# Decode-attention forward: the engines' order taken from the scheduler and written by hand, with three heads in flight

## Chip, cores, metric

One Trainium2 chip (trn2), one core. The metric is the device time of one launch in microseconds (us). An execution that is over 1.5% above the fastest of its kernel would be set aside as slow. The profile is one execution of the same program; its span is about 2 us shorter than the timed launch.

The engines are named as the profile names them: PE (matmul; PEld are its weight loads), DVE (vector), ACT (scalar), POOL, SP (it issues the loads). "DMA share" is the mean busy share of the core's 16 DMA engines.

## The reference, cut to what matters

A conditioned layer norm, one decode step of attention over a long cache, an MLP, and the gradients of all of it. Only the attention's forward is touched by the change: 32 heads, one query token, a cache of 8192 keys and values of 192 numbers per head, in bf16.

```python
q = (h @ wq) per head                            # 32 heads x 192
scores = einsum(q, k_cache) * 192 ** -0.5        # 8192 per head
p = softmax(scores)
o = einsum(p, v_cache)                           # 192 per head
x = x + ga * (o @ wo)
# then an MLP block, and vjp: gradients for k_cache, v_cache, wq, wo, w3, w4, ...
```

K and V are 201 MB together and are read once in the forward. The gradients of K and V are as large again; they are written by the backward, which reads V a second time.

## The kernel before

Per head, 8192 keys lie as 128 partitions x 64. The forward of a head has these steps; the line numbers are those that the profile shows.

```python
def dot_mul(src, vec, halve, psR):                         # half of a head's K
    prod = pp.tile(...)                                    # ONE buffer of 12 KB per partition
    V_.tensor_tensor(out=prod, in0=src, in1=vec, op=mult)              # L266, DVE 3.36 us
    V_.tensor_tensor(out=prod[lo], in0=prod[lo], in1=prod[hi], op=add) # L270, DVE 1.75 us
    ps = psR.tile(...)
    for k in range(0, w, TS):                              # "the tree": 6 matmuls, 1.4 us
        T_.matmul(ps, lhsT=ident_bf, rhs=prod[:, :, k:k+TS], ...)      # L273, PE
    return ps

def softmax(h, S_h):        # reduce_max m1 (DVE), max matmul mx (PE), negm (DVE),
    ...                     # E4 = exp(S_h + negm) and two copies (ACT, 1.0 us)

def scale_v(q, v, E4, Ef):  # vs = E * V for a quarter of the keys: 7 of 16 rows on ACT
    ...                     # (2.6 us with a small copy), 9 of 16 on DVE (1.05 us)

def m_quarter(q, kb, vs, mp, op):   # PE, 2.7 us: mp += K^T vs (L330, L334), op += 1^T vs (L338)

for i in range(HQ + 1):                          # program text, not yet the engines' order
    # ... loads of head i; mp, op for head i-1
    if new: d0 = dot_mul(kh[0], qh, True, psR)
    quarter(0)                                   # scale_v and m_quarter of head i-1
    if new: d1 = dot_mul(kh[1], qh, True, psR); dot_sum(d0, ...)
    quarter(1)
    if new: dot_sum(d1, ...); E4, Ef = softmax(i, S_h)
    quarter(2); quarter(3)
    # every 4th head: q_chunk (the next 4 heads' q) or mod_blocks; 10 such chunks in all
    if old: m_out(...)                           # copies of mp, op (ACT), one add (DVE)
            # every 2nd head: pair_out (10 small fp32 matmuls into po, reciprocal rz,
            # 15 matmuls ao_ps, copy AO on ACT) and e_rows (a transpose, a copy, a store)
```

A scheduling layer decides in which order these instructions stand on each engine. PE, DVE and ACT then take them in that order: the Trainium skill, "TensorE: Matmul & The Clock Gate", Part 1 ("Engine queue depths"), calls ACT's and DVE's queues strict FIFO and says that PE can pull weight loads ahead of matmuls.

Of the kernel before, what the change touches and what calls it, by code (L numbers as in the profile page):

```python
# [8 lines left out]
FP32 = mybir.dt.float32  # L9
BF16 = mybir.dt.bfloat16  # L10
ALU = mybir.AluOpType
# [9 lines left out]
def kernel(  # L21
# [26 lines left out]
    nc = tc.nc  # L48
# [62 lines left out]
    def tcol(n, name, dtype=FP32):  # L111
        return tmp.tile([P, n], dtype, name=name)
# [147 lines left out]
        nc.sync.dma_start(out=v, in_=V_hd[h][:, t * JH : (t + 1) * JH, :])  # L260
        return v

    def dot_mul(src, vec, halve, psR):

        prod = pp.tile([P, JH, DH], BF16, name="prod", tag="prod")
        V_.tensor_tensor(out=prod, in0=src, in1=vec[:, None, :].to_broadcast([P, JH, DH]), op=ALU.mult)  # L266
        w = DH
        if halve:
            w //= 2
            V_.tensor_tensor(out=prod[:, :, 0:w], in0=prod[:, :, 0:w], in1=prod[:, :, w : 2 * w], op=ALU.add)  # L270
        ps = psR.tile([P, JH, TS], FP32, name="dot_ps")
        for k in range(0, w, TS):
            T_.matmul(ps, lhsT=ident_bf, rhs=prod[:, :, k : k + TS], start=(k == 0), stop=(k == w - TS))  # L273
        return ps

    def dot_sum(ps, dst):
        V_.reduce_sum(out=dst, in_=ps, axis=AX.X)  # L277
# [5 lines left out]
    with tc.tile_pool(name="kp", bufs=1) as kp, tc.tile_pool(name="vs", bufs=3) as vsp, tc.tile_pool(name="ft", bufs=2) as ft, \  # L283
# [9 lines left out]
            nc.sync.dma_start(out=kb, in_=K_hd[h][:, t * JH : (t + 1) * JH, :])  # L293
            return kb

        def softmax(h, S_h):
            m1 = tcol(1, "m1")
            V_.reduce_max(out=m1, in_=S_h, axis=AX.X)
            mx = psB.tile([P, P], FP32, name="mx", tag="b")
            T_.matmul(mx, lhsT=m1[:, 0:1].to_broadcast([P, P]), rhs=ident_f, start=True, stop=True)  # L300
            negm = tcol(1, "negm")
            V_.reduce_max(out=negm, in_=mx, axis=AX.X, negate=True)
            E4 = ft.tile([P, J, 4], BF16, name="E4")
            A_.activation(out=E4, in_=S_h[:, :, None].to_broadcast([P, J, 4]), func=ACT.Exp, bias=negm[:, 0:1], scale=1.0)
            A_.copy(out=E_all[:, h, :], in_=E4[:, :, 0])
            Ef = ft.tile([P, J], FP32, name="Ef")
            A_.copy(out=Ef, in_=E4[:, :, 0])
            return E4, Ef
# [28 lines left out]
                p0 = 32 * (k % 4)  # L337
                T_.matmul(op[p0 : p0 + 32, 0:MW], lhsT=ones_bf, rhs=vs[:, k, 0:MW], start=(q == 0 and k < 4), stop=(z and k >= JQ - 4), skip_group_check=True)  # L338

        def m_out(h, mp, op):  # L340
            t, b = divmod(h, 2)
            A_.copy(out=M1[:, h, :], in_=mp[:, 0:MW])  # L342
            mt = ft.tile([P, MW], FP32, name="mt", bufs=1)
            A_.copy(out=mt[64:128, :], in_=mp[64:128, MO : MO + MW])
            V_.tensor_tensor(out=M2[64 * b : 64 * b + 64, t, :], in0=mp[0:64, MO : MO + MW], in1=mt[64:128, :], op=ALU.add)
            osb = ft.tile([P, MW], FP32, name="osb")
            A_.copy(out=osb, in_=op[:, 0:MW])
            return osb

        def e_rows(t):  # L350
            ps = psS.tile([P, P], BF16, name="er_ps", tag="s")
            T_.transpose(out=ps[0 : 2 * J, :], in_=E_all[:, 2 * t : 2 * t + 2, :].rearrange("p h j -> p (h j)"), identity=ident_bf)
            er = ft.tile([P, P], BF16, name="er", bufs=1)
            A_.copy(out=er[0 : 2 * J, :], in_=ps[0 : 2 * J, :])
            nc.scalar.dma_start(out=eT_d[2 * t * J : (2 * t + 2) * J, :], in_=er[0 : 2 * J, :])

        def pair_out(t, os2, wo_t):

            po = psS.tile([P, 8], FP32, name="po", tag="s")
            for b in range(2):  # L360
                rows = slice(64 * b, 64 * b + 64)
                for k in range(3):
                    T_.matmul(po[rows, k : k + 1], lhsT=os2[b][:, k:DH:3], rhs=c32[:, 0:1], start=True, stop=True)
                T_.matmul(po[rows, 3:4], lhsT=c32[:, 0:64], rhs=os2[b][:, DH:MW], start=True, stop=True)
                T_.matmul(po[:, 4 + b : 5 + b], lhsT=c32, rhs=os2[b][:, DH:MW], start=True, stop=True)
            rz = tcol(3, "rz")
            V_.reciprocal(out=rz, in_=po[:, 3:6])
            V_.tensor_scalar(out=o_col[:, 3 * t : 3 * t + 3], in0=po[:, 0:3], scalar1=rz[:, 0:1], scalar2=None, op0=ALU.mult)
            V_.tensor_copy(out=rinv[:, 2 * t : 2 * t + 2], in_=rz[:, 1:3])
            o2 = ft.tile([P, 3, 2], BF16, name="o2")  # L370
            V_.tensor_tensor(out=o2, in0=omask, in1=o_col[:, 3 * t : 3 * t + 3, None].to_broadcast([P, 3, 2]), op=ALU.mult)
            ps = psS.tile([P, ND, 2], FP32, name="ao_ps", tag="s")
            for i in range(ND):
                for k in range(3):
                    T_.matmul(ps[:, i, :], lhsT=wo_t[:, k, i * P : (i + 1) * P], rhs=o2[:, k, :], start=(k == 0), stop=(k == 2))
            A_.copy(out=AO[:, :, 2 * t : 2 * t + 2], in_=ps)

        st, os_, wo_l = {}, {}, {}
        q_chunk(0, load_w(wq_v, 0, CW))
        mb = MB0  # L380
        for i in range(HQ + 1):
            new, old = i < HQ, i > 0
            if new:
                kh = [load_k(i, 0), load_k(i, 1)]
                vh = [load_v(i, 0)]
                S_h = ft.tile([P, J], FP32, name="S_h")
                qh = qs_bc[:, i * DH : (i + 1) * DH]
                if i % 2 == 0:
                    wo_l[i // 2] = load_wo(i // 2)
            if old:  # L390
                pk, pv, pE4, pEf = st.pop(i - 1)
                mp = psM.tile([P, 512], FP32, name="mp")
                op = psO.tile([P, 256], FP32, name="op")

            def quarter(q):
                if old:
                    m_quarter(q, pk[q // 2], scale_v(q, pv[q // 2], pE4, pEf), mp, op)

            if new:
                d0 = dot_mul(kh[0], qh, True, psR)  # L400
            quarter(0)
            if new:
                d1 = dot_mul(kh[1], qh, True, psR)
                dot_sum(d0, S_h[:, 0:JH])
            quarter(1)
            if new:
                vh.append(load_v(i, 1))
                dot_sum(d1, S_h[:, JH:J])
                E4, Ef = softmax(i, S_h)
                st[i] = (kh, vh, E4, Ef)  # L410
            quarter(2)
            quarter(3)
            if i % 4 == 3 and i + 1 < HQ:
                q_chunk((i + 1) // 4, load_w(wq_v, ((i + 1) // 4) * CW, ((i + 1) // 4 + 1) * CW))
            if i % 4 == 1 and mb < NMB:
                nb = min(CW // P, NMB - mb)
                mod_blocks(mb, nb, load_w(wm_v, mb * P, (mb + nb) * P))
                mb += nb
            if old:
                os_[i - 1] = m_out(i - 1, mp, op)  # L420
                if i % 2 == 0:
                    t = (i - 2) // 2
                    pair_out(t, (os_.pop(i - 2), os_.pop(i - 1)), wo_l.pop(t))
                    e_rows(t)
        while mb < NMB:
            nb = min(CW // P, NMB - mb)
            mod_blocks(mb, nb, load_w(wm_v, mb * P, (mb + nb) * P))
            mb += nb
    V_.tensor_tensor(out=dbo, in0=dy_c, in1=gb, op=ALU.mult)


# [123 lines left out]
    with tc.tile_pool(name="bk1", bufs=1) as bk1, tc.tile_pool(name="ob", bufs=4) as ob, tc.tile_pool(name="bst", bufs=1) as bst:  # L555
# [166 lines left out]
        for h in range(HQ):  # L722
            doh = do_bc[:, h * DH : (h + 1) * DH]
            qh = qs_bc[:, h * DH : (h + 1) * DH]
            for t in range(2):
                js = slice(t * JH, (t + 1) * JH)
                v = load_v(h, t)
                dP = tcol(JH, "dP")
                dot_sum(dot_mul(v, doh, False, psR), dP)
                dS4 = bst.tile([P, JH, 4], BF16, name="dS4", bufs=2)  # L730
                V_.scalar_tensor_tensor(
                    out=dS4,
                    in0=dP[:, :, None].to_broadcast([P, JH, 4]),
                    scalar=cpr[:, h : h + 1],
                    in1=E_all[:, h, js, None].to_broadcast([P, JH, 4]),
                    op0=ALU.subtract,
                    op1=ALU.mult,
                )
                dV = ob.tile([P, JH, DH], BF16, name="dV", tag="o")
                outer_v(dV, load_er(h, t), doh)  # L740
                nc.gpsimd.dma_start(out=dV_hd[h][:, js, :], in_=dV)  # L741
                dK = ob.tile([P, JH, DH], BF16, name="dK", tag="o")
                times(dK, qh, dS4, 0, JH)
                nc.gpsimd.dma_start(out=dK_hd[h][:, js, :], in_=dK)
                for f in side.get(2 * h + t, ()):
                    f()
# [35 lines left out]
```

## Time and profile before

| | before |
|---|---|
| median, 4 runs | 1719.45 us (1716.70 to 1722.35) |
| forward: last copy of the last head ends | 780.2 us |
| mean time between two heads' negm | 23.5 us |
| backward: from its first multiply to the end | 873.4 us |

The windows view of the kernel before. The columns are the stretch, its length, the busy us of each engine with its number of instructions, the granted PE clock (1.00 is full), the DMA share and GB/s:

```profile
26.00:762.00 736.00, 603.10 (x7102) 409.15 (x7101) 512.96 (x468) 390.51 (x1225) 0.00 (x0) 0.86 0.74 295
839.40:1712.80 873.40, 657.67 (x4095) 228.18 (x4093) 559.41 (x665) 478.72 (x651) 91.32 (x158) 0.59 0.96 386
```

In the forward (first line) no engine is full: PE is busy 82%, DVE 70%, ACT 53%, and the loads have a share of 0.74. The backward (second line) is bound by its transfers at a share of 0.96. So the time that an order can win lies in the forward.

The waits view of the forward before, 30 to 762 us: who waited for whom, us in total, times, longest (S_h is the tile of the head's scores):

```profile
DVE prod L266 <- PE dot_ps L273: 121.9, 31, 5.3
DVE S_h L277 <- PE dot_ps L273: 46.9, 32, 2.8
DVE negm L302 <- PE mx L300: 21.4, 31, 1.0
...
ACT M_212 L342 <- PE mp L334: 148.2, 31, 6.5
ACT AO L376 <- PE ao_ps L375: 66.3, 15, 6.7
```

DVE waits 3.9 us a time for a tree before it may overwrite the one product buffer. The timeline of DVE shows why, for one head (start, length, then the wait in brackets):

```profile
302.64 0.29 DVE L302 TENSOR_REDUCE negm<-mx 128x1 f32<-128x128 f32 x1 [0.89 <-PE mx L300]
303.51 3.00 DVE L316 TENSOR_TENSOR vs<-v_sb,E_3592 128x1728 bf16<-128x1728 bf16 x3 [0.58 <-ACT E_3592 L304]
306.42 3.35 DVE L266 TENSOR_TENSOR prod<-KB_237,qs_bc 128x6144 bf16<-128x6144 bf16 x1
...
310.66 1.75 DVE L270 TENSOR_TENSOR prod<-prod 128x3072 bf16<-128x3072 bf16 x1
316.26 3.36 DVE L266 TENSOR_TENSOR prod<-KB_238,qs_bc 128x6144 bf16<-128x6144 bf16 x1 [3.85 <-PE dot_ps L273]
```

and on PE the tree that it waits for, which could have begun at 312.4:

```profile
304.71 1.77 PE L330 MATMUL mp<-vs,KB_240 128*128 128x193 bf16 x10
...
311.98 1.52 PE L330 MATMUL mp<-vs,KB_241 128*128 128x193 bf16 x16
...
314.76 1.46 PE L273 MATMUL dot_ps<-prod,ident_bf 128*128 128x512 bf16 x6
```

The tree stands behind M quarters of the head whose softmax has just ended. The first of them began at 304.71, a microsecond after the scaling of V did (303.51), and the scaling had waited for that softmax. One head's chain (softmax, scaling, M) and the next head's chain (multiply, fold, tree) are thus tied into one loop; DVE and PE cannot run ahead of each other.

### The profile page before, as it was taken

The numbers are of one execution on the slowest core, as the hardware profiler recorded it, in microseconds if no ns is written. First come the engines' busy times: TensorE is split into PE (matmuls) and PEld (weight loads), VectorE is DVE, ScalarE is ACT, GpSimd is POOL, SyncE is SP. The second block draws the span as 40 slices with busy tenths as digits, with TensorE's granted clock in tenths as the row PEclk, the third lists the DMA queues.
The fourth block names the chain that finished last, engine by engine and source line by source line (L and its number), as shares of the span: only waits on it lengthen the run. The fifth ranks groups of instructions, "written<-read, shape, count | busy, mean of one in ns | idle before, by whom it ended". The sixth has DMA issues, their size and how long they took to land.

```text
span 1712.8 us, 28289 instructions
## 1 busy us (share of the span) xinstructions
PE 1311.6 (77%) x11811; PEld 675.5 (39%) x11811; DVE 1114.0 (65%) x1273; ACT 900.0 (53%) x1948; POOL 99.9 (6%) x177
## 2 busy tenths in 40 slices
PE   4888778888888888786558587887678888878774
PEld 2555555555555655555223132232222222222211
DVE  5666666767767776764557566666756666666664
ACT  2455544555555555553456365555555555555554
POOL 0000000000000000000101010111010101010111
PEclk9888878888888888886667665556665555555555
DMA  8787577777787777765489999999999999999988
GB/s 347 321 324 309 226 315 279 295 280 295 283 324 307 292 286 286 288 235 201 178 353 414 379 382 409 396 400 424 424 377 402 392 405 369 373 397 396 409 342 336
DMA packets 78270, 576.00 MB, mean 336 GB/s; under 512 B 9374, under 2 KB 27118, under 8 KB 37182
## 3 DMA queue, kind: packets, MB, share of 16 engines
q1 hardware_dynamic: 51530, 347.23, 51.2%
q0 software_dynamic: 23776, 225.92, 32.2%
q8 instruction: 92, 1.51, 0.4%
q10 hardware_dynamic: 2836, 1.05, 0.2%
q14 instruction: 36, 0.29, 0.0%
HBM read 347.74 MB, written 226.43 MB: 335 GB/s over the span
## 4 chain that ended last, share of the span: by engine, by line
PE 40%; issue 23%; DVE 14%; DMA 12%; ACT 7%; POOL 2%; SPq 0%; POOLq 0%; ACTq 0%; DVEq 0%
PE dot_ps L273 14%; PE mp L330 10%; DVE prod L266 7%; DMA v_sb<-in_A_v_cache_dram 4%; PE mp L334 4%; PE op L338 3%; PE dv_ps L682 3%; ACT vs L323 3%; DVE prod L270 3%; DMA w_st<-in_A_wq_dram 2%; ACT dV L683 2%; PE wT_ps L573 2%; DMA wo_st<-in_A_wo_dram 2%; DMA w_st<-in_w_mod_dram 1%; DVE S_h L277 1%
## 5 line engine op out<-in xcount | busy, mean ns | idle before, releaser
L273 PE MATMUL dot_ps<-prod,ident_bf 128*128 128x512 bf16 x1152 | 475.0, 542 | 87.1 <-DVE prod L270 46.6
L683 ACT CAST dV<-dv_ps 128x768 bf16<-128x768 f32 x512 | 388.2, 811 | 205.7 <-PE dv_ps L682 186.6
L323 ACT ACTIVATE vs<-v_sb,Ef 128x192 bf16<-128x192 bf16 x896 | 325.8, 448 | 0.0
L682 PE MATMUL dv_ps<-do_bc,er_b 1*128 1x192 bf16 x2048 | 219.6, 324 | 64.8 <-ACT dV L683 64.0
L273 PEld LDWEIGHTS <-ident_bf 128*128 128x128 bf16 x1152 | 119.4, 117 | 264.7 <-issue 233.9
L266 DVE TENSOR_TENSOR prod<-v_sb,do_bc 128x6144 bf16<-128x6144 bf16 x64 | 214.3, 3349 | 3.5 <-ACT do_bc L624 3.5
L277 DVE TENSOR_REDUCE dP<-dot_ps 128x32 f32<-128x512 f32 x64 | 44.2, 691 | 235.5 <-PE dot_ps L273 235.5
L682 PEld LDWEIGHTS <-er_b 1*128 1x128 bf16 x2048 | 65.2, 102 | 300.5 <-issue 296.7
L270 DVE TENSOR_TENSOR prod<-prod 128x3072 bf16<-128x3072 bf16 x64 | 112.0, 1750 | 0.0
L338 PE MATMUL op<-vs,ones_bf 128*32 128x193 bf16 x2048 | 102.6, 264 | 0.0
L573 PE MATMUL wT_ps<-ident_bf,w_st 128*128 128x128 bf16 (+1 forms) x470 | 50.7, 285 | 66.4 <-ACT wqT L574 25.8
L342 ACT COPY M_212<-mp 128x193 f32<-128x193 f32 x32 | 10.3, 322 | 152.5 <-PE mp L334 152.5
L574 ACT COPY wqT<-wT_ps 128x1024 bf16<-128x1024 bf16 (+1 forms) x52 | 50.6, 973 | 49.2 <-PE wT_ps L573 35.1
L277 DVE TENSOR_REDUCE S_h<-dot_ps 128x32 f32<-128x512 f32 x64 | 44.0, 688 | 46.9 <-PE dot_ps L273 46.9
L741 POOL DMA_DIRECT2D out_dram<-dV x64 | 35.4, 553 | 658.2 <-ACT dV L683 635.1
L573 PEld LDWEIGHTS <-w_st 128*128 128x128 bf16 (+1 forms) x470 | 36.8, 130 | 86.5 <-issue 47.5
L266 DVE TENSOR_TENSOR prod<-KB_238,qs_bc 128x6144 bf16<-128x6144 bf16 x13 | 43.6, 3355 | 28.8 <-PE dot_ps L273 23.9
L338 PEld LDWEIGHTS <-ones_bf 128*32 128x32 bf16 x2048 | 43.4, 96 | 46.4 <-issue 29.0
L266 DVE TENSOR_TENSOR prod<-KB_241,qs_bc 128x6144 bf16<-128x6144 bf16 x13 | 43.6, 3356 | 27.4 <-PE dot_ps L273 27.4
L266 DVE TENSOR_TENSOR prod<-KB_239,qs_bc 128x6144 bf16<-128x6144 bf16 x13 | 43.6, 3356 | 27.3 <-PE dot_ps L273 27.3
L330 PE MATMUL mp<-vs,KB_238 128*128 128x193 bf16 x416 | 52.6, 275 | 10.6 <-DVE vs L316 6.3
L330 PE MATMUL mp<-vs,KB_240 128*128 128x193 bf16 x416 | 52.3, 275 | 10.6 <-DVE vs L316 8.4
(653 smaller groups left out, 1760.2 us busy)
## 6 DMA issues: line engine op xcount, KB each, us to landing
v_sb<-in_A_v_cache_dram SPq DMA_DIRECT2D x128, 1536.0 KB
out_dram<-dV POOLq DMA_DIRECT2D x64, 1536.0 KB, 8.9
out_dram<-dK POOLq DMA_DIRECT2D x64, 1536.0 KB, 13.0
KB_238<-in_A_k_cache_dram SPq DMA_DIRECT2D x13, 1536.0 KB
KB_239<-in_A_k_cache_dram SPq DMA_DIRECT2D x13, 1536.0 KB
KB_240<-in_A_k_cache_dram SPq DMA_DIRECT2D x13, 1536.0 KB
KB_241<-in_A_k_cache_dram SPq DMA_DIRECT2D x13, 1536.0 KB
KB_237<-in_A_k_cache_dram SPq DMA_DIRECT2D x12, 1536.0 KB
```

The source lines that it names most:

```text
L266: V_.tensor_tensor(out=prod, in0=src, in1=vec[:, None, :].to_broadcast([P, JH, DH]), op=ALU.mult)
L270: V_.tensor_tensor(out=prod[:, :, 0:w], in0=prod[:, :, 0:w], in1=prod[:, :, w : 2 * w], op=ALU.add)
L273: T_.matmul(ps, lhsT=ident_bf, rhs=prod[:, :, k : k + TS], start=(k == 0), stop=(k == w - TS))
L277: V_.reduce_sum(out=dst, in_=ps, axis=AX.X)
L323: A_.activation(out=vs[:, k, 0:DH], in_=v[:, v0 + k, :], func=ACT.Copy, scale=Ef[:, j0 + k : j0 + k + 1])
L330: T_.matmul(mp[:, 0:MW], lhsT=kb[:, j0 + k, 0:P], rhs=vs[:, k, 0:MW], start=(q == 0 and k == 0), stop=(z and k == JQ - 1), skip_group_chec ...
L334: T_.matmul(mp[p0 : p0 + 64, MO : MO + MW], lhsT=kb[:, j0 + k, P:DH], rhs=vs[:, k, 0:MW], start=False, stop=(z and k >= JQ - 2), skip_grou ...
L338: T_.matmul(op[p0 : p0 + 32, 0:MW], lhsT=ones_bf, rhs=vs[:, k, 0:MW], start=(q == 0 and k < 4), stop=(z and k >= JQ - 4), skip_group_check ...
L573: T_.transpose(out=tp[lo:hi, (x - x0) * P : (x - x0 + 1) * P], in_=src, identity=ident_bf)
L574: A_.copy(out=wT[:, x0 * P : (x0 + n) * P], in_=tp[:, 0 : n * P])
L682: T_.matmul(ps[:, b, k * DH : (k + 1) * DH], lhsT=er[p0 : p0 + 1, 2 * m + k, :], rhs=doh[p0 : p0 + 1, :], start=True, stop=True)
L683: A_.copy(out=dV4[:, 2 * q : 2 * q + 2, m * PW : (m + 1) * PW], in_=ps[:, :, 0:PW])
```

## The change

Its intent: write the order of PE, DVE and ACT by hand, so that work of three heads stands side by side. In iteration i, head i has its dots, head i-1 its softmax and M quarters 0 to 2, and head i-2 its M quarter 3. The diff, cut to its core (the helpers are only split so that their parts can be placed one by one):

```diff
-    def dot_mul(src, vec, halve, psR):         # multiply, fold and tree in one
+    def dot_mul(src, vec): ...                 # multiply
+    def dot_half(prod): ...                    # fold
+    def dot_tree(prod, psR, w): ...            # tree
...
-            nc.scalar.dma_start(out=eT_d[...], in_=er[...])
+            nc.gpsimd.dma_start(out=eT_d[...], in_=er[...])
...
-        for i in range(HQ + 1):
+        with tc.manual_schedule(engines={PE, DVE, Activation}):
+            for i in range(HQ + 2):            # x: head i, y: head i-1, z: head i-2
+                ...                            # loads of x
+                if y: dot_sum(y["d1"], ...); m1 = reduce_max(y["S"])
+                if x: pa = dot_mul(x["k"][0], qh)
+                if y: mx = matmul(m1 ...)
+                if z: m_quarter(3, z["k"][1], z["vs"], ...)
+                if y: negm = reduce_max(mx, negate); E4, Ef = softmax(i - 1, ...)
+                if x: dot_half(pa); x["d0"] = dot_tree(pa, ...)          # "tree a"
+                if y: vs = scale_v(0, ...)
+                if z: mt = m_out(i - 2, ...)
+                if y: m_quarter(0, ...)
+                if x: pb = dot_mul(x["k"][1], qh)                        # second multiply
+                if z: m_add(i - 2, ...)
+                if y: vs = scale_v(1, ...); m_quarter(1, ...)
+                if last: po = pair_sums(...)                             # i odd
+                if x: dot_half(pb); x["d1"] = dot_tree(pb, ...)          # "tree b"
+                if y: vs = scale_v(2, ...); m_quarter(2, ...)
+                if last: o2 = pair_o(t, po)
+                         A_.copy(out=AO[...], in_=pair_ao(o2, ...)); e_rows_out(...)
+                if wch: q_chunk(...) or mod_blocks(...)                  # i odd
+                if x: dot_sum(x["d0"], ...)
+                if y: y["vs"] = scale_v(3, ...)                          # used one head later
```

More of the change, by code (lines that the diff above doesn't have):

```diff
@@ L261, in load_v, with dot_mul, dot_half, dot_tree @@
         return v
-    def dot_mul(src, vec, halve, psR):
+    def dot_mul(src, vec):
         prod = pp.tile([P, JH, DH], BF16, name="prod", tag="prod")
         V_.tensor_tensor(out=prod, in0=src, in1=vec[:, None, :].to_broadcast([P, JH, DH]), op=ALU.mult)
-        w = DH
-        if halve:
-            w //= 2
-            V_.tensor_tensor(out=prod[:, :, 0:w], in0=prod[:, :, 0:w], in1=prod[:, :, w : 2 * w], op=ALU.add)
+        return prod
+    def dot_half(prod):
+        w = DH // 2
+        V_.tensor_tensor(out=prod[:, :, 0:w], in0=prod[:, :, 0:w], in1=prod[:, :, w : 2 * w], op=ALU.add)
+    def dot_tree(prod, psR, w):
         ps = psR.tile([P, JH, TS], FP32, name="dot_ps")
@@ L294, in load_k, with softmax @@
             return kb
-        def softmax(h, S_h):
-            m1 = tcol(1, "m1")
-            V_.reduce_max(out=m1, in_=S_h, axis=AX.X)
-            mx = psB.tile([P, P], FP32, name="mx", tag="b")
-            T_.matmul(mx, lhsT=m1[:, 0:1].to_broadcast([P, P]), rhs=ident_f, start=True, stop=True)
-            negm = tcol(1, "negm")
-            V_.reduce_max(out=negm, in_=mx, axis=AX.X, negate=True)
+        def softmax(h, S_h, negm):
             E4 = ft.tile([P, J, 4], BF16, name="E4")
@@ L338, in m_quarter, with m_out @@
                 T_.matmul(op[p0 : p0 + 32, 0:MW], lhsT=ones_bf, rhs=vs[:, k, 0:MW], start=(q == 0 and k < 4), stop=(z and k >= JQ - 4), skip_group_check=True)
-        def m_out(h, mp, op):
-            t, b = divmod(h, 2)
+        def m_out(h, mp, op, os_):
             A_.copy(out=M1[:, h, :], in_=mp[:, 0:MW])
@@ L344, in m_out, with m_add @@
             A_.copy(out=mt[64:128, :], in_=mp[64:128, MO : MO + MW])
+            os_[h] = ft.tile([P, MW], FP32, name="osb")
+            A_.copy(out=os_[h], in_=op[:, 0:MW])
+            return mt
+        def m_add(h, mp, mt):
+            t, b = divmod(h, 2)
             V_.tensor_tensor(out=M2[64 * b : 64 * b + 64, t, :], in0=mp[0:64, MO : MO + MW], in1=mt[64:128, :], op=ALU.add)
-            osb = ft.tile([P, MW], FP32, name="osb")
-            A_.copy(out=osb, in_=op[:, 0:MW])
-            return osb
         def e_rows(t):
@@ L352, in e_rows, with e_rows_out, pair_sums @@
             T_.transpose(out=ps[0 : 2 * J, :], in_=E_all[:, 2 * t : 2 * t + 2, :].rearrange("p h j -> p (h j)"), identity=ident_bf)
+            return ps
+        def e_rows_out(t, ps):
             er = ft.tile([P, P], BF16, name="er", bufs=1)
             A_.copy(out=er[0 : 2 * J, :], in_=ps[0 : 2 * J, :])
-            nc.scalar.dma_start(out=eT_d[2 * t * J : (2 * t + 2) * J, :], in_=er[0 : 2 * J, :])
-        def pair_out(t, os2, wo_t):
+            nc.gpsimd.dma_start(out=eT_d[2 * t * J : (2 * t + 2) * J, :], in_=er[0 : 2 * J, :])
+        def pair_sums(os2):
             po = psS.tile([P, 8], FP32, name="po", tag="s")
@@ L365, in pair_out, with pair_o @@
                 T_.matmul(po[:, 4 + b : 5 + b], lhsT=c32, rhs=os2[b][:, DH:MW], start=True, stop=True)
+            return po
+        def pair_o(t, po):
             rz = tcol(3, "rz")
@@ L371, in pair_out, with pair_ao @@
             V_.tensor_tensor(out=o2, in0=omask, in1=o_col[:, 3 * t : 3 * t + 3, None].to_broadcast([P, 3, 2]), op=ALU.mult)
+            return o2
+        def pair_ao(o2, wo_t):
             ps = psS.tile([P, ND, 2], FP32, name="ao_ps", tag="s")
@@ L375, in pair_out @@
                     T_.matmul(ps[:, i, :], lhsT=wo_t[:, k, i * P : (i + 1) * P], rhs=o2[:, k, :], start=(k == 0), stop=(k == 2))
-            A_.copy(out=AO[:, :, 2 * t : 2 * t + 2], in_=ps)
-        st, os_, wo_l = {}, {}, {}
+            return ps
+        ORDER = {mybir.EngineType.PE, mybir.EngineType.DVE, mybir.EngineType.Activation}
         q_chunk(0, load_w(wq_v, 0, CW))
         mb = MB0
-        for i in range(HQ + 1):
-            new, old = i < HQ, i > 0
-            if new:
-                kh = [load_k(i, 0), load_k(i, 1)]
-                vh = [load_v(i, 0)]
-                S_h = ft.tile([P, J], FP32, name="S_h")
-                qh = qs_bc[:, i * DH : (i + 1) * DH]
-                if i % 2 == 0:
-                    wo_l[i // 2] = load_wo(i // 2)
-            if old:
-                pk, pv, pE4, pEf = st.pop(i - 1)
-                mp = psM.tile([P, 512], FP32, name="mp")
-                op = psO.tile([P, 256], FP32, name="op")
-            def quarter(q):
-                if old:
-                    m_quarter(q, pk[q // 2], scale_v(q, pv[q // 2], pE4, pEf), mp, op)
-            if new:
-                d0 = dot_mul(kh[0], qh, True, psR)
-            quarter(0)
-            if new:
-                d1 = dot_mul(kh[1], qh, True, psR)
-                dot_sum(d0, S_h[:, 0:JH])
-            quarter(1)
-            if new:
-                vh.append(load_v(i, 1))
-                dot_sum(d1, S_h[:, JH:J])
-                E4, Ef = softmax(i, S_h)
-                st[i] = (kh, vh, E4, Ef)
-            quarter(2)
-            quarter(3)
-            if i % 4 == 3 and i + 1 < HQ:
-                q_chunk((i + 1) // 4, load_w(wq_v, ((i + 1) // 4) * CW, ((i + 1) // 4 + 1) * CW))
-            if i % 4 == 1 and mb < NMB:
@@ new lines @@
+        X, os_, wo_l = {}, {}, {}
+        with tc.manual_schedule(engines=ORDER):
+            for i in range(HQ + 2):
+                x = X[i] = {} if i < HQ else None
+                y = X.get(i - 1) if 0 < i <= HQ else None
+                z = X.pop(i - 2) if i > 1 else None
+                wch = None
+                if x is not None:
+                    x["k"] = [load_k(i, 0), load_k(i, 1)]
+                    x["v"] = [load_v(i, 0)]
+                    x["S"] = ft.tile([P, J], FP32, name="S_h")
+                    qh = qs_bc[:, i * DH : (i + 1) * DH]
+                    if i % 2 == 0:
+                        wo_l[i // 2] = load_wo(i // 2)
+                if i % 4 == 3 and i + 1 < HQ:
+                    wch = load_w(wq_v, ((i + 1) // 4) * CW, ((i + 1) // 4 + 1) * CW)
+                if i % 4 == 1 and mb < NMB:
+                    nb = min(CW // P, NMB - mb)
+                    wch = load_w(wm_v, mb * P, (mb + nb) * P)
+                if y is not None:
+                    dot_sum(y["d1"], y["S"][:, JH:J])
+                    m1 = tcol(1, "m1")
+                    V_.reduce_max(out=m1, in_=y["S"], axis=AX.X)
+                if x is not None:
+                    pa = dot_mul(x["k"][0], qh)
+                if y is not None:
+                    mx = psB.tile([P, P], FP32, name="mx", tag="b")
+                    T_.matmul(mx, lhsT=m1[:, 0:1].to_broadcast([P, P]), rhs=ident_f, start=True, stop=True)
+                if z is not None:
+                    m_quarter(3, z["k"][1], z["vs"], z["mp"], z["op"])
+                if y is not None:
+                    negm = tcol(1, "negm")
+                    V_.reduce_max(out=negm, in_=mx, axis=AX.X, negate=True)
+                    E4, Ef = softmax(i - 1, y["S"], negm)
+                if x is not None:
+                    dot_half(pa)
+                    x["d0"] = dot_tree(pa, psR, DH // 2)
+                if y is not None:
+                    y["mp"] = psM.tile([P, 512], FP32, name="mp")
+                    y["op"] = psO.tile([P, 256], FP32, name="op")
+                    vs = scale_v(0, y["v"][0], E4, Ef)
+                if z is not None:
+                    mt = m_out(i - 2, z["mp"], z["op"], os_)
+                if y is not None:
+                    m_quarter(0, y["k"][0], vs, y["mp"], y["op"])
+                if x is not None:
+                    pb = dot_mul(x["k"][1], qh)
+                if z is not None:
+                    m_add(i - 2, z["mp"], mt)
+                if y is not None:
+                    vs = scale_v(1, y["v"][0], E4, Ef)
+                    m_quarter(1, y["k"][0], vs, y["mp"], y["op"])
+                if x is not None:
+                    x["v"].append(load_v(i, 1))
+                last = z is not None and i % 2 == 1
+                t = (i - 3) // 2
+                if last:
+                    po = pair_sums((os_.pop(i - 3), os_.pop(i - 2)))
+                if x is not None:
+                    dot_half(pb)
+                    x["d1"] = dot_tree(pb, psR, DH // 2)
+                if y is not None:
+                    vs = scale_v(2, y["v"][1], E4, Ef)
+                    m_quarter(2, y["k"][1], vs, y["mp"], y["op"])
+                if last:
+                    o2 = pair_o(t, po)
+                    A_.copy(out=AO[:, :, 2 * t : 2 * t + 2], in_=pair_ao(o2, wo_l.pop(t)))
+                    e_rows_out(t, e_rows(t))
+                if wch is not None:
+                    if i % 4 == 3:
+                        q_chunk((i + 1) // 4, wch)
+                    else:
+                        mod_blocks(mb, nb, wch)
+                        mb += nb
+                if x is not None:
+                    dot_sum(x["d0"], x["S"][:, 0:JH])
+                if y is not None:
+                    y["vs"] = scale_v(3, y["v"][1], E4, Ef)
+            while mb < NMB:
@@ L418 @@
                 mb += nb
-            if old:
-                os_[i - 1] = m_out(i - 1, mp, op)
-                if i % 2 == 0:
-                    t = (i - 2) // 2
-                    pair_out(t, (os_.pop(i - 2), os_.pop(i - 1)), wo_l.pop(t))
-                    e_rows(t)
-        while mb < NMB:
-            nb = min(CW // P, NMB - mb)
-            mod_blocks(mb, nb, load_w(wm_v, mb * P, (mb + nb) * P))
-            mb += nb
     V_.tensor_tensor(out=dbo, in0=dy_c, in1=gb, op=ALU.mult)
@@ L728 @@
                 dP = tcol(JH, "dP")
-                dot_sum(dot_mul(v, doh, False, psR), dP)
+                dot_sum(dot_tree(dot_mul(v, doh), psR, DH), dP)
                 dS4 = bst.tile([P, JH, 4], BF16, name="dS4", bufs=2)
```

## The prediction, made before the changed kernel ran

> **What bounds it now.** The windows view: forward (26–762 us) takes 736 us for 32 heads, 23.0 each; no engine is full: PE 82%, DVE 70%, ACT 53%, DMA share 0.74 at 295 GB/s, granted clock 0.86. The backward (850–1713) is DMA-bound (share 0.96, 388 GB/s), and the order view says its instructions are unchanged. So the gain must come from the forward.
>
> The timeline of 300–348 us shows a latency loop per head: reduce_max, max matmul, negm, E4 exp (1.0 us on ACT), four scaled quarters of V (2.6 us each on ACT, 1.05 on DVE), while the dot tree of K's second half stands on PE behind M quarters that wait for V. The waits view (100–740, 28 heads): DVE waits 106 us for the tree before reusing the single prod tile, 40 for the tree before S_h, 19 for mx; ACT waits 126 us for M's last quarter before copying M1 and about 6.5 per head for negm; PE waits 32 for prod, 25 for vs.
>
> **What the change does.** No work is added or removed; the 16 small E-row stores go to the POOL queue (0.33 us each off ACT). Softmax and M quarters 0–2 run one head after the dots, M quarter 3 two, so exp and the scaling of V run beside the next head's dots.
>
> **Worked estimate, from trace durations.** Per head DVE needs about 16 us (2×3.3 multiply, 2×1.7 fold, 4×1.0 vs, small rest), ACT 13, PE 4×2.7 for M + 2×1.4 trees + 0.5 = 14, plus 2.2 on every second head for the pair and 2.5 more for a q or mod chunk. Walking the new order: an even head loses 0.5 us on DVE to tree a (prod still has one buffer). In an odd head the pair's AO copy stands on ACT before the last scaled quarter and waits for PE's M quarter 2 and ao_ps; so vs 3 ends late, the next head's M quarter 3 too, and tree a and the second multiply wait 2–3 us. That gives 37.9 us per pair, plus about 3 us at each of 10 chunk iterations, where the max matmul stands behind the chunk: 19.9 per head.
>
> DMA: 7.0 MB per head. The first 30 us ran at 372 GB/s, share 0.95, so the floor is about 18 us per head. K half 1 is freed by M quarter 1 and needed about 12 us later, as long as a load in the chain of waits takes (11.8–14 us). The Trainium skill ("DMA: Bandwidth & Descriptors", Specifications) gives a 435 GB/s ceiling; this trace reaches 424. I add 0.4 us per head for late loads: 20.3.
>
> Forward saving 32×(23.0−20.3) = 86 us, plus a few at the ends. Predicted **1632 us**, range 1592–1678. Chances: faster by over 2% 0.91, within 2% 0.07, slower 0.02.
>
> **What shows it right.** Forward end (last osb copy) near 690 us, not 780; there DVE busy 80%, DMA share 0.88, about 345 GB/s. ACT's wait of M1 for PE gone; DVE's wait for trees 1–2 us per head; largest new waits ACT AO on ao_ps and DVE negm on mx in odd heads. Backward within 1% of 863 us.
>
> **What would make it wrong.** Late loads (multiply waiting for KB): DMA then sets 21–22 us per head. In-order PE with a stalled quarter blocking the tree more than I walked; the clock staying low. Better: the odd-head chain hidden, giving 18 us, near 1575.

## The result and the profile after

| | before | after |
|---|---|---|
| median, 4 runs each | 1719.45 us | 1627.50 us (1626.37 to 1641.15) |
| ratio, 95% interval | | 0.9483 (0.9428 to 0.9538) |
| last copy of the last head ends | 780.2 us | 689.3 us |
| mean time between two heads' negm | 23.5 us | 20.5 us |
| backward, first multiply to the end | 873.4 us | 875.9 us |

A ratio here and below is the mean time of one kernel's fast runs over that of the kernel before in the same rounds, so it is not quite the ratio of the medians.

The windows view of the kernel after, forward and backward:

```profile
26.00:669.00 643.00, 533.09 (x6988) 393.58 (x6988) 509.21 (x468) 381.33 (x1212) 7.73 (x14) 0.92 0.84 335
748.80:1624.70 875.90, 663.23 (x4097) 230.26 (x4095) 559.95 (x665) 478.65 (x652) 90.88 (x158) 0.58 0.96 385
```

DVE's busy time in the forward is what it was (513 and 509 us), now in 643 us instead of 736. The whole gain, 91 us, is there by the end of the forward; the backward is unchanged within 0.3%. DVE's waits, summed over all causes from 30 us up to the last head's negm, fell from 220.6 to 133.5 us, which is nearly all of it.

One thing changed with the order that no run separates from it: the granted PE clock in the forward rose from 0.86 to 0.92, and PE's busy time for the same 11811 matmuls fell from 1311.6 to 1251.1 us over the whole program. PE's steps in the loop became shorter too; how much of the 91 us came that way stays open.

The waits view of the forward after, 30 to 670 us:

```profile
DVE rz L372 <- PE po L367: 42.0, 15, 4.1
DVE prod L265 <- PE dot_ps L276: 24.2, 27, 1.8
DVE prod L265 <- ACT qs_bc L245: 20.6, 5, 5.1
DVE S_h L280 <- PE dot_ps L276: 19.1, 14, 2.2
DVE prod L265 <- DMA KB<-in_A_k_cache_dram: 13.2, 7, 3.3
...
DVE negm L423 <- PE mx L418: 1.6, 4, 0.4
...
ACT AO L457 <- PE ao_ps L383: 131.7, 14, 12.6
```

The wait for the product buffer fell from 121.9 to 24.2 us, and ACT's wait to copy M1 (148.2 us before) is not in the list any more. Two stand out now: ACT waits 9.4 us at each AO copy (4.4 before), and DVE, newly, 2.8 us at each reciprocal rz. The chain of waits around one odd head shows where the first leads; it runs forward in time, start, length, what:

```profile
340.72 0.47 PE ao_ps L383 x15
341.21 0.18 ACT AO L457
...
341.65 0.83 PE q_ps L243 x5
342.50 0.50 ACT qs_bc L245
...
343.04 0.99 PE q_ps L243 x5
...
344.67 2.44 ACT vs L320 x7
...
348.63 1.42 PE dot_ps L276 x6
350.06 3.36 DVE prod L265
```

The AO copy and the chunk's copies stand on ACT before the scaled quarter 3 of V (vs L320). That quarter is ready to be made long before, but it is made last; then come the late M quarter 3 of this head, tree a of the next head, and the second multiply, at 350.06. This is the chain that the prediction walked. How much it costs cannot be read from this head: its second multiply waited only 0.76 us for tree a, because DVE was late already, its first multiply having waited for K:

```profile
343.12 3.36 DVE L265 TENSOR_TENSOR prod<-KB,qs_bc 128x6144 bf16<-128x6144 bf16 x1 [3.21 <-DMA KB<-in_A_k_cache_dram]
...
350.06 3.36 DVE L265 TENSOR_TENSOR prod<-KB,qs_bc 128x6144 bf16<-128x6144 bf16 x1 [0.76 <-PE dot_ps L276]
```

The experiment vs3_before_ao below measures it.

### The profile page after: what moved, and what is told of

The parts are those of the page before. It is cut to its first block, busy times and chain, and to the rows that moved or that the text cites. A ratio compares the mean times of both kernels' runs of the same rounds, so it can differ in the third digit from the quotient of the medians.

```text
span 1624.7 us, 28236 instructions
## 1 busy us (share of the span) xinstructions
PE 1251.1 (77%) x11811; PEld 665.3 (41%) x11811; DVE 1110.5 (68%) x1273; ACT 894.3 (55%) x1948; POOL 108.0 (7%) x193
## 4 chain that ended last, share of the span: by engine, by line
issue 35%; PE 28%; DVE 18%; DMA 8%; ACT 6%; POOL 4%; SPq 0%; POOLq 0%; ACTq 0%; DVEq 0%
DVE prod L265 10%; PE dot_ps L276 10%; PE mp L327 6%; PE mp L331 3%; ACT vs L320 3%; DMA w_st<-in_w_mod_dram 2%; DVE vs L313 2%; DMA KB<-in_A_k_cache_dram 2%; PE op L335 2%; DMA out_dram<-dK 2%; DVE prod L270 2%; POOL out_dram L788 1%; POOL out_dram L785 1%; PE po L365 1%; PE dv_ps L726 1%
## 5 line engine op out<-in xcount | busy, mean ns | idle before, releaser
L320 ACT ACTIVATE vs<-v_sb,Ef 128x192 bf16<-128x192 bf16 x896 | 323.3, 443 | 0.0
L327 PE MATMUL mp<-vs,KB 128*128 128x193 bf16 x2048 | 229.9, 265 | 80.7 <-DVE vs L313 72.8
L265 DVE TENSOR_TENSOR prod<-KB,qs_bc 128x6144 bf16<-128x6144 bf16 x64 | 214.7, 3355 | 65.8 <-PE dot_ps L276 27.1
L327 PEld LDWEIGHTS <-KB 128*128 128x128 bf16 x2048 | 193.8, 105 | 117.5 <-DVE vs L313 80.6
L731 DVE TENSOR_TENSOR dK<-qs_bc,dS 128x6144 bf16<-128x6144 bf16 x64 | 214.2, 3346 | 10.5 <-DMA out_dram<-dK 10.4
L313 DVE TENSOR_TENSOR vs<-v_sb,E 128x1728 bf16<-128x1728 bf16 x128 | 134.5, 1052 | 7.8 <-ACT E L301 7.3
L331 PE MATMUL mp<-vs,KB 128*64 128x193 bf16 x2048 | 116.0, 259 | 0.0
L331 PEld LDWEIGHTS <-KB 128*64 128x64 bf16 x2048 | 87.5, 114 | 27.4 <-issue 27.4
L301 ACT ACTIVATE E<-S_h,negm 128x256 bf16<-128x256 f32 x32 | 16.1, 502 | 103.6 <-DVE negm L423 103.6
```

The lines of the kernel that those rows point to most:

```text
L265: V_.tensor_tensor(out=prod, in0=src, in1=vec[:, None, :].to_broadcast([P, JH, DH]), op=ALU.mult)
L313: V_.tensor_tensor(out=vs[:, 0:n, 0:DH].rearrange("p j (a b) -> p j a b", b=4), in0=v[:, v0 : v0 + n, :].rearrange("p j (a b) -> p j a b", ...
L320: A_.activation(out=vs[:, k, 0:DH], in_=v[:, v0 + k, :], func=ACT.Copy, scale=Ef[:, j0 + k : j0 + k + 1])
L327: T_.matmul(mp[:, 0:MW], lhsT=kb[:, j0 + k, 0:P], rhs=vs[:, k, 0:MW], start=(q == 0 and k == 0), stop=(z and k == JQ - 1), skip_group_chec ...
L331: T_.matmul(mp[p0 : p0 + 64, MO : MO + MW], lhsT=kb[:, j0 + k, P:DH], rhs=vs[:, k, 0:MW], start=False, stop=(z and k >= JQ - 2), skip_grou ...
L731: V_.tensor_tensor(out=out3[:, n0_:n1_, :].rearrange("p j (a b) -> p j a b", b=4), in0=vec.rearrange("p (a b) -> p a b", b=4)[:, None, :, ...
```

## Experiments

Two questions: where does the gain come from, and what is left? All kernels were timed in three rounds against the kernel before on the same chip. The runs came in batches on different chips, where the kernel before took 1714.78 to 1719.45 us; a difference of medians between batches can be off by that much, and the ratios are the better guide. All but the two marked ones gave correct results. The counts of matmuls (11811), DVE (1273) and ACT (1948) instructions are equal on the pages of the before, changed, auto_order, old_order_by_hand, quarter3_same_head, sums_early, two_moves and three_moves kernels: those differ in order alone (and in the queue of 16 small stores).

| run | median us | ratio to before, 95% |
|---|---|---|
| (changed kernel) | 1627.50 | 0.9483 (0.9428–0.9538) |
| auto_order | 1723.89 | 1.0020 (0.9982–1.0059) |
| old_order_by_hand | 1891.84 | 1.1003 (1.0977–1.1029) |
| quarter3_same_head | 1675.62 | 0.9743 (0.9718–0.9769) |
| erows_on_act | 1634.94 | 0.9517 (0.9467–0.9568) |
| vs3_before_ao | 1606.84 | 0.9352 (0.9310–0.9394) |
| sums_early | 1592.26 | 0.9257 (0.9220–0.9293) |
| chunk_even | 1648.70 | 0.9593 (0.9551–0.9634) |
| two_moves | 1574.45 | 0.9179 (0.9165–0.9193) |
| three_moves | 1560.28 | 0.9071 (0.9047–0.9094) |
| three_moves_loads_in_order | 1556.99 | 0.9083 (0.9064–0.9102) |
| three_moves_half_v (wrong results) | 1541.30 | 0.8988 (0.8973–0.9003) |
| changed_half_v (wrong results) | 1620.65 | 0.9459 (0.9433–0.9485) |

### Is it the hand order, or the program's new stages? auto_order

```diff
-        with tc.manual_schedule(engines=ORDER):
+        if True:
```

> The changed program with its hand order taken off: the scheduler orders the three engines again. The order view shows that it puts the exp, the four scaled quarters and M back in front of the next head's dots (three vs before the multiply, the tree behind M quarters), almost as in the kernel before. Theory (the gain needs the hand order; splitting the stages in the program alone gives nothing): 1700 to 1735 us, forward about 23 us per head. Rival (the gain comes from the program's new stages, whoever orders them): 1620 to 1660.

Measured: 1723.89 us, the time of the kernel before. The order view (no time in it) shows one head on DVE, left as the scheduler orders the new program, right as written by hand (the pair's small instructions left out):

```
scheduler                              by hand
S_h, m1, negm                          S_h, m1
vs x3          (head i-1)              multiply a     (head i)
multiply a     (head i)                negm           (head i-1)
vs             (head i-1)              fold a, vs, multiply b
fold a, multiply b                     vs, fold b, vs
S_h, fold b                            S_h, vs
```

The scheduler brings the three scalings forward to the softmax that releases them, as it did before the change, and the old waits come back with it (waits view of auto_order, 30 to 650 us):

```profile
DVE prod L265 <- PE dot_ps L276: 106.8, 26, 5.2
DVE S_h L280 <- PE dot_ps L276: 41.9, 26, 2.8
```

So the stages in the program text do nothing by themselves; the gain needs the written order.

### Is any written order enough? old_order_by_hand

```diff
+        with tc.manual_schedule(engines={PE, DVE, Activation}):
             for i in range(HQ + 1):            # the loop of the kernel before, unchanged
```

> The kernel before, whose forward loop is kept in program order on the three engines, nothing else changed. Theory (the gain comes from work of three heads standing side by side): walking the order with trace durations, M's add at the end of each head waits on DVE for M quarter 3 and its copy, about 5 us per head, negm waits about 2: 24 to 26 us per head, 1740 to 1800 us. Rival (the scheduler's order was the whole fault, any written order mends it): 1640 to 1680.

Measured: 1891.84 us, 10% slower than before, and slower than the theory's own range. Its waits view, 30 to 650 us (22 of the 32 heads):

```profile
ACT E L304 <- DVE negm L302: 272.7, 22, 17.3
DVE M L345 <- ACT mt L344: 156.1, 20, 10.8
DVE negm L302 <- PE mx L300: 50.2, 22, 2.3
```

The waits that the expectation named are there (M's add 7.1 us per head, negm 2.3). The walk missed what ACT does: the exp of head i stands on ACT before the scaled quarters 2 and 3 of head i-1, so ACT waits 12.4 us per head for negm and only then scales, which makes M's end later still. A written order is worth as much as its walk through all three engines.

### Is the quarter that runs two heads late needed? quarter3_same_head

```diff
-                if z is not None:
-                    m_quarter(3, z["k"][1], z["vs"], z["mp"], z["op"])
 ...
                 y["vs"] = scale_v(3, y["v"][1], E4, Ef)
+                m_quarter(3, y["k"][1], y["vs"], y["mp"], y["op"])
```

> The changed kernel with M quarter 3 at the end of its own head's iteration, before the max matmul of the next softmax, not one later. Theory: PE then holds mx until vs 3 is scaled; negm waits 1 to 5 us and the second multiply 1 to 2.5 more; about 2 us per head: 1670 to 1700 us. Rival (the late quarter is a detail): 1620 to 1640.

Measured: 1675.62 us, in the theory's range. Of the changed kernel's gain of 5.2% half (2.6%) is left. Its waits view, 30 to 650 us, has the named wait, which was 1.6 us in all in the changed kernel:

```profile
DVE negm L421 <- PE mx L418: 64.6, 27, 5.7
```

PE holds the next softmax's max matmul behind an M quarter that waits for scaled V. Run one head later, that quarter stands behind the max matmul instead, and its inputs are older. The second multiply's part was smaller than expected: up to the last negm its waits for tree a rose from 24.2 us in all to 33.9, some 0.3 us per head.

### Is the store's queue part of it? erows_on_act

```diff
-            nc.gpsimd.dma_start(out=eT_d[...], in_=er[...])
+            nc.scalar.dma_start(out=eT_d[...], in_=er[...])
```

> The changed kernel with the 16 stores of E rows back on the ACT queue. Theory: 16 x 0.33 us on an engine with room: within 6 us, 1622 to 1634 us. Rival (the queue is part of the gain): over 10 us slower.

Measured: 1634.94 us, 1 us above the theory's range; the intervals of the two ratios (0.9467–0.9568 and 0.9428–0.9538) overlap almost wholly. No effect can be told from noise here. That fits the Trainium skill, "DMA: Bandwidth & Descriptors", "Issuing engines are not separate DMA queues": the choice of the issuer saves only the issuer's own time, 0.33 us per store in the trace of the kernel before.

### What is left: the three moves, together and one by one

The chain of waits of the changed kernel and its waits view named three suspects. The moves:

```diff
 # vs3_before_ao: the scaled quarter 3 ahead of the AO copy (and the chunk's copies) on ACT
                 if last: o2 = pair_o(t, po)
+                if y is not None: y["vs"] = scale_v(3, y["v"][1], E4, Ef)
                 if last: A_.copy(out=AO[...], in_=pair_ao(o2, ...)); e_rows_out(...)
 ...
-                if y is not None: y["vs"] = scale_v(3, y["v"][1], E4, Ef)
 # sums_early: the pair's 10 small matmuls between M quarters 0 and 1 on PE
                 if y is not None: m_quarter(0, ...)
+                if last: po = pair_sums(...)
                 if x is not None: pb = dot_mul(x["k"][1], qh)
                 if y is not None: vs = scale_v(1, ...); m_quarter(1, ...)
-                if last: po = pair_sums(...)
 # chunk_even: q and mod chunks in the even heads, one head earlier
-                if i % 4 == 3: q chunk for head i+1
+                if i % 4 == 2: q chunk for head i+2
-                if i % 4 == 1: mod chunk
+                if i % 4 == 0 and i > 0: mod chunk
```

> A version meant to beat both: the scaled quarter 3 stands before the pair's AO copy on ACT, the pair's sums stand before M quarter 1 on PE, and the q and mod chunks fall in the even heads, one head earlier. Theory (what is left is these waits: rz for po 42 us, multiply for qs 21, late vs 3 before tree a): 18.5 to 19 us per head, 1575 to 1600 us, DMA share about 0.93 in the forward. Rival (loads already set the pace at a share of 0.84): 1610 to 1630 with the multiply waiting for K instead.

Measured: 1560.28 us, below the expected range: 4.3% off the changed kernel (0.9071/0.9483 = 0.957), 9.3% off the kernel before. It is correct and beats both. The windows view of its forward:

```profile
26.00:602.00 576.00, 497.63 (x6994) 376.49 (x6994) 506.33 (x467) 385.35 (x1220) 7.71 (x14) 0.97 0.94 373
```

DVE is now busy 88%, the PE clock is granted at 0.97, and the loads have a share of 0.94. One by one:

> The changed kernel with one of the three moves: the scaled quarter 3 of V stands before the pair's AO copy on ACT (with the chunk's copies after it too). The three together took 67 us off 1627.5. Theory (vs 3 held behind the AO copy, which waits 132 us in all for ao_ps, delays M quarter 3, tree a and the second multiply of the next head): 20 to 30 us off, 1597 to 1608 us. Rival (that wait is off the path, ACT has room): 1620 to 1630.

Measured: 1606.84 us, 20.7 off, in the range. The quarter's place behind the AO copy was on the path. But the loss did not fall mainly where it was expected. Two waits views, 30 to 650 us; of the changed kernel, SP's (L260 is V's load):

```profile
SPq L260 <- ACT vs L320: 122.3, 31, 10.5
```

and of this run, SP's and DVE's:

```profile
SPq L260 <- ACT vs L320: 4.8, 12, 0.5
...
DVE prod L265 <- PE dot_ps L276: 21.3, 31, 1.8
DVE S_h L280 <- PE dot_ps L276: 10.4, 7, 2.2
DVE prod L265 <- DMA KB<-in_A_k_cache_dram: 6.6, 2, 3.4
```

The wait for tree a fell by 3 us only (from 24.2); those for tree b (from 19.1) and for K (from 13.2) fell by more. The late quarter had also held V's buffer, and with it the next load of V. That the K waits came from K loads standing behind those V loads fits this, but no run isolates it.

> The changed kernel with one move: the pair's ten small matmuls stand before M quarter 1 on PE, in the gap where PE waits for vs 1. Theory: DVE's wait of rz for po (42 us in all) goes, but part of the time comes back where DVE then waits for a late vs 3 and tree a: 10 to 25 us off, 1603 to 1618 us. Rival (all of it is on the path): 40 off, 1587.

Measured: 1592.26 us, 35.2 off: more than the theory, near the rival's 40. The waits of rz for po are gone from its list. Between 30 and 650 us some of it came back (S_h's wait for tree b went from 18.8 to 31.1 us, the multiply's for K from 12.3 to 23.4), and half as much went elsewhere (its wait for qs from 20.6 to 9.0). The 35.2 us are what was left of the 42 after these; they are not the price of rz alone.

> The changed kernel with one move: q and mod chunks in the even heads, one head earlier. Theory (the multiply's wait for qs, 20.6 us in 5 waits, goes; the chunk's 2.5 us on PE falls in a head without the pair): 15 to 25 us off, 1602 to 1613 us. Rival (the wait moves to the max matmul, which stands behind the chunk in either place): 1620 to 1630.

Measured: 1648.70 us, 21 us slower: the sign was wrong. The wait for qs is gone from DVE's list, but ACT's timeline in an even head shows a new one (chunk_even):

```profile
250.11 0.49 ACT L245 ACTIVATE qs_bc<-q_ps 128x384 bf16<-128x384 f32 x1 [6.11 <-PE q_ps L243]
...
252.18 2.53 ACT L320 ACTIVATE vs<-v_sb,Ef 128x192 bf16<-128x192 bf16 x7
```

The chunk's copies stand on ACT before the scaled quarter 3, like the AO copy in odd heads. Alone, the move thus puts the late quarter into the even heads too. Three of DVE's waits grew (30 to 650 us; in the changed kernel 24.2, 12.3 and 1.6):

```profile
DVE prod L265 <- PE dot_ps L276: 38.4, 27, 1.8
DVE prod L265 <- DMA KB<-in_A_k_cache_dram: 30.9, 8, 5.6
...
DVE negm L423 <- PE mx L418: 10.4, 11, 1.9
```

The third is what the rival had named, so it was right in part. If the late quarter is the main reason, the same move must help once the scaled quarter 3 stands ahead. That is what two_moves tests (the first two moves, chunks left in odd heads):

> The changed kernel with the scaled quarter 3 before the AO copy and the pair's sums before M quarter 1, chunks left in the odd heads. Alone these took 20.7 and 35.2 us off 1627.5, the chunk move alone added 21. Theory (the chunk move did harm alone only because its copies stood before the scaled quarter 3 on ACT, in a second head; with that quarter moved ahead it helps): 1566 to 1582 us, slower than the three moves at 1560. Rival (chunks in even heads always harm): 1530 to 1550.

Measured: 1574.45 us, in the theory's range. So the chunk move costs 21 us alone and gains 14 us (1574.45 to 1560.28; by the ratios 19) after the other two. Effects of moves in an order need not add up: -20.7, -35.2 and +21.2 sum to -34.7, and together they gave -67.2. The first two nearly do: -55.9 as a sum, -53.1 together.

### Do the loads set the pace? The runs with half of V, and with the loads in order

```diff
-                    x["v"].append(load_v(i, 1))
+                    x["v"].append(x["v"][0])           # wrong results on purpose
```

> Wrong results on purpose: the changed kernel, with V's second half not loaded in the forward and the first half used twice. The prediction put late loads at 0.4 us per head (13 us in all); the profile shows the multiply waiting 13 us for K. Theory: 8 to 25 us off, 1602 to 1620 us. Rival (the loads at a share of 0.84 set the pace): 1550 to 1580.

Measured: 1620.65 us, 7 us less in the median, and the ratio intervals overlap (0.9433–0.9485 and 0.9428–0.9538). With 22% of the forward's bytes gone the changed kernel is hardly faster: its loads, at a share of 0.84, do not set its pace.

> Wrong results on purpose: the three moves, with V's second half not loaded in the forward; the first half is used twice, so 22% of the forward's bytes are gone and no instruction else. Theory (with the moves the loads set the pace at 18.4 us per head; without them the DVE's order needs 16.7 to 17): 1505 to 1522 us. Rival (waits among the engines remain): 1545 to 1560.

Measured: 1541.30 us, 19 us less in the median and 14 by the ratios, so in this version late loads do cost, about 0.5 us per head. But the theory is refuted as to size: the time between heads went from 18.4 to 17.9 us, not to 16.7–17. Its waits view, 30 to 600 us, without any wait for loads on DVE:

```profile
DVE prod L265 <- PE dot_ps L276: 24.0, 31, 1.8
DVE negm L423 <- PE mx L418: 16.2, 8, 2.8
DVE S_h L280 <- PE dot_ps L276: 12.5, 11, 2.2
```

These remain: tree a before the product buffer is free (0.7 to 1.2 us per head in all versions of the changed kernel's written order), the max matmul behind a chunk, and tree b behind M quarter 1.

> The three moves with the load queue in written order too: each K and V load stands in the order in which its buffer comes free, where the scheduler had put V behind a late buffer in front of the next K in every fourth head or so (one multiply waited 6.1 us for K). Theory (28 us of waits for K come from that order): 10 to 22 us off, 1538 to 1551 us. Rival (the loads are at their pace, share 0.94, 373 GB/s in the forward): 1553 to 1563.

The edit adds SP to the engines kept in written order and issues each K and V load where its buffer comes free. Measured: 1556.99 us, and the ratio (0.9083) is that of three_moves (0.9071) within the intervals: no gain, the rival was right. DVE's waits for K did fall, from 28.2 us to 9.2 (30 to 600 us), but its waits for mx and for tree b rose from 13.8 us together to 32.4. At a share of 0.94 there was little left to win, and another wait took its place.

What stays open: a second product buffer would take the 24 us of tree a away. It was not tried: with the other pools as they are, the pool of scaled V no longer fits (the build reports that it needs 18.4 KB per partition and 11.9 are left). And a better hand order of the old two-head stages was not tried; old_order_by_hand is one order, the program's.

## Why the prediction was right, point by point

The predicted 1632 us against 1627.5 measured is right, and mostly for the stated reasons. Some of its terms were off in opposite directions; that the sum came so near is in part luck.

- **The gain lies in the forward, the backward stays.** Right: forward end 689.3 us (predicted near 690), backward within 0.3% (within 1%).
- **The loop of softmax, scaling and tree is what the change opens.** Right: the wait for the product buffer fell from 3.8 us per head to 0.8 (121.9/32, 24.2/32; predicted 1–2 for all waits on trees; with S_h's 19.1 it is 1.4). quarter3_same_head and auto_order show that both the late quarter and the written order are needed. The prediction did not ask whether the scheduler would have done it; auto_order answered no.
- **The odd-head chain through the AO copy.** Right that it is on the path: AO's wait for ao_ps doubled (66.3 to 131.7 us) and became ACT's largest, and vs3_before_ao took 20.7 us off. Wrong as to where: 2–3 us were expected at tree a and the second multiply of each such head, but the longest of these waits was 1.8 us, and with the quarter moved ahead they fell by 3 us in all. More was saved at tree b and at the loads of K.
- **37.9 us per pair without a chunk, 3 us more with one.** The first term was too small, the second too large. From the negm times of the changed kernel, the five pairs from heads 13 to 30 without a chunk took 40.3 us on average (the last of them only 37.1), the nine with one 42.0. The wait that the prediction does not name at all is rz for po, 2.8 us per pair (42.0/15); taking it away in sums_early gained 35.2 us, net of what came back elsewhere.
- **"The max matmul stands behind the chunk" and "DVE negm on mx" as a large new wait.** Wrong as named: negm waited for mx 1.6 us in all. The chunk was felt as the next head's multiply waiting for the q that the chunk makes (20.6 us in 5 waits), and through the late scaled quarter. The data dependence was overlooked.
- **0.4 us per head for late loads.** The wait came as predicted: the multiply waited 13.2 us for K, 0.4 per head. What it cost is not shown: changed_half_v bought 7 us, 0.2 per head, not told from noise.
- **The sum.** The measured pairs contain the late loads, so 40.3 us stand against 37.9 + 0.8: an underestimate of some 1.6 x 16 = 26 us. The chunks' overestimate (1.3 x 10 = 13 us) made up for half of it, so that 20.3 us per head were predicted and 20.5 measured. The share came to 0.84 and 335 GB/s (predicted 0.88 and 345), and DVE to 79% (80%).

## What to carry to other kernels

Where no engine is full and each stands still by turns, look for a loop of two chains on engines that take their instructions in order, and ask of each waiting instruction what ready work stands behind it on the same engine. The same counts of instructions took 1892, 1724, 1676, 1628 or 1560 us here, by order alone. A move of one instruction must be walked on every engine that it touches: the same chunk move cost 21 us or gained 14, depending on what stood behind its copies. And splitting a program into pipeline stages may do nothing while a scheduler still decides the order; look at the order that came out.

## What the Trainium skill lacked or had wrong

- "TensorE: Matmul & The Clock Gate", Part 1 ("HAM oscillation"), tells the reader to avoid PE idle gaps over about 3.4 us. That shorter ones can matter, the same page says in "A second HAM failure mode", but without a length. In the changed kernel PE stood 2.32 us for scaled V, and in the 2.6 us after it the granted clock was 0.57 and the 16 matmuls of an M quarter took 2.55 us; after another gap, of 2.33 us, the same 16 took 1.52. The length of the gap alone thus does not tell. The free-running window of which the page speaks in Part 1 may explain both; no run here tests that. The two quarters in the changed kernel's timeline, then its windows view of the stretch after the first gap:

```profile
313.68 2.55 PE L327 MATMUL mp<-vs,KB 128*128 128x193 bf16 x16 [2.32 <-DVE vs L313]
331.97 1.52 PE L327 MATMUL mp<-vs,KB 128*128 128x193 bf16 x16 [2.33 <-DVE vs L313]
```

```profile
313.60:316.20 2.60, 2.52 (x18) 2.09 (x20) 2.60 (x4) 2.60 (x9) 0.00 (x0) 0.57 0.98 408
```

- "DMA: Bandwidth & Descriptors", Specifications, lists an HBM limit of about 358 GB/s per core as half of the stack's rate. Only further down, under its table of measurements, does the page say that this is the share with both cores of a pair busy. This program, which runs on one core, moved 373 GB/s over the 576 us of three_moves' forward. "HBM Reference", Specifications, has it right (about 425 GB/s for a core alone).
- "Perfetto Trace Analysis", "Identifying Performance Opportunities", says to find the most-contended engine and optimize it first, by finding what blocks it in its gaps. A stretch where none is full (82%, 70%, 53%, share 0.74 here) it calls latency-bound, under its roofline table; that the order of instructions on the engines is then a thing to change, it does not say (it speaks of interleaving whole regimes). Order alone gave 9% here. No page tells how to check an order that a scheduler chose.
